# The last 64 keys' values on all 128 rows beside zeros, and every block of 128 tokens through the MLP by itself

## The chip, the cores and the metric

The program runs on one core of one Trainium2 chip. The metric is the device time of one execution in microseconds (us). The engines go by their short names: PE (TensorE; PEld is its weight loads), DVE (VectorE), ACT (ScalarE), POOL (GpSimd), SP (SyncE, which here issues DMAs).

## The reference

Three stages in float32: attention that keeps the 32 largest scores of every row, a SwiGLU MLP behind an RMS norm, and a top-1 mixture of 8 experts.

```python
q, k, v: (4, 8, 576, 64)                       # batch, heads, tokens, head size
scores = q @ k.T / 8;  keep the 32 largest of each row;  attn = softmax @ v
x  = attn as (2304, 512)
xn = x / rms(x) * g
x  = (silu(xn @ w_gate) * (xn @ w_val)) @ w_out            # 512 -> 1536 -> 512
e  = argmax(x @ gate + bias[modality])                     # one of 8 experts per token
out = gate_weight * (relu(x @ w1[e]) @ w2[e])              # 512 -> 1024 -> 512
```

## The kernel before

**Stages.** `front` computes attention and MLP together; `experts` follows. The last MLP output has to be there before the experts start, since the table that says which token goes to which expert is complete only then.

**Tiling of attention.** A sequence of 576 tokens is four blocks of 128 rows (`CM = 4`) and a rest of 64 (`SR`). A *main tile* is 128 query rows of one head. A *rest tile* holds the 64 rest rows of two heads. A *step* takes two tiles, and there are 72 steps, 18 for each of the 4 batches. `PLAN` (line 93) is the order: for batches 0, 1 and 3 the blocks come one at a time, 4 steps for each; in batch 2 blocks 0 and 1 come together, in 8 steps, whose two tiles are the two blocks of one head. "r" stands for the two steps of the rest tiles. Where the two tiles of a step are one block, they are the two heads (`hh` = 0 and 1) of a pair `p`.

**One tile.** `qk` (L530) makes the scores: 4 matmuls, 8 for a rest tile. ACT and DVE copy and halve them (L543 to L547), `topk` (L565, L568) finds the 32 largest on DVE (for each tile four searches for 8 maxima and three removals), `soft1` to `soft3` (POOL L599, ACT) make the weights, `tr` (L625) transposes them, ACT, POOL and DVE write them as two 16-bit halves (`pT` for the 512 main keys, `pr` for the 64 rest keys), and `av` (L671) multiplies them with the values. Float32 is replaced by three 16-bit products (high by high, high by low, low by high); the tiles of pairs 2 and 3 of batch 0 use float32 itself (`whole`).

**The rest keys.** The two tiles of a step lie in one buffer, so that the rest keys of both are neighbours and one transpose (L630) gives `pr` of both: rows 0 to 63 belong to the even tile, rows 64 to 127 to the odd one. So `av` takes 64 rows of `pr` and 64 rows of the values; the 64 rest rows of the values are loaded twice (L388), once for each half. In a rest tile each head's 64 columns are matmuls of their own, with 64 of the array's columns.

**MLP.** A *granule* is one block (or the two blocks of batch 2's first 8 steps; or the rest rows of two batches). Its atoms are `norm`, `xtr`, `ff1` (L750, rows named `pf`: 144 matmuls with w_gate and 144 with w_val for one block), `ff2` (L750, rows named `po`: 72), `route` and `rank` (together some 20 short DVE instructions). A granule of one block streams 128 columns per `ff1` matmul, the granule of two blocks 256 and half as many matmuls for its tokens.

**What sets the order.** Atoms are written into the attention steps by a budget (`mlp_slot`), but a scheduler then orders every engine's instructions by its own simulation of the program. Each engine runs its queue in that order. `w` has 2 buffers and the scores' PSUM tile 1, so a step's scores can be made about one step ahead of the top-k that uses them. `kr` and `vt` share one buffer (tag "raw") outside `whole`.

Of the kernel before, what the change touches and what calls it, by code (L numbers as in the profile page):

```python
# [20 lines left out]
def topk_attention_swiglu_moe_kernel(  # L21
# [192 lines left out]
    def front(exact):  # L214
# [219 lines left out]
        def dma_q(s):  # L434
            qr = ap_.tile([128, 2, D], F32, name="qr", tag="qr", bufs=QB)
            t0, t1 = steps[s]
            b, p, hh, c = t0
            if hh is not None and t1[2] == hh:
                src = q[b, 2 * p + hh, 0:SM, :].rearrange("(p c) d -> p c d", c=CM)
                nc.sync.dma_start(out=qr, in_=src[:, c:c + 2, :])  # L440
            else:
                for t, (b, p, hh, c) in enumerate(steps[s]):
                    if hh is not None:
                        src = q[b, 2 * p + hh, 0:SM, :].rearrange("(p c) d -> p c d", c=CM)
                        nc.sync.dma_start(out=qr[:, t, :], in_=src[:, c, :])
                    else:
                        for i in range(2):
                            nc.sync.dma_start(out=qr[i * SR:(i + 1) * SR, t, :], in_=q[b, 2 * p + i, SM:S, :])
# [905 lines left out]
```

## Time and profile before

| | us |
|---|---|
| median of 3 runs (lowest, highest) | 1242.8 (1239.47, 1243.44) |
| the profiled execution | 1240.91, of it span 1239.3 |
| PE busy in the span | 1138.8 |
| DVE busy | 928.2 |
| ACT busy | 830.5 |
| POOL busy | 731.2 |

The first score matmul of step 18 (batch 1's first) starts at 220.3, that of step 21 at 277.2, that of step 71 (the last) at 803.5; attention's last matmul is at 833.4, the MLP's last at 926.8, and the experts take the rest. The page marks 92% of the span as PE busy, but the ends of matmuls are modelled, so a busy PE need not be one that is kept from starting sooner: the distance between the starts of weight loads shows what each one takes.

### The profile page before, as it was taken

The numbers are of one execution on the slowest core, as the hardware profiler recorded it, in microseconds if no ns is written. First come the engines' busy times: TensorE is split into PE (matmuls) and PEld (weight loads), VectorE is DVE, ScalarE is ACT, GpSimd is POOL, SyncE is SP. The second block draws the span as 40 slices with busy tenths as digits, with TensorE's granted clock in tenths as the row PEclk, the third lists the DMA queues.
The fourth block names the chain that finished last, engine by engine and source line by source line (L and its number), as shares of the span: only waits on it lengthen the run. The fifth ranks groups of instructions, "written<-read, shape, count | busy, mean of one in ns | idle before, by whom it ended". The sixth has DMA issues, their size and how long they took to land. (4 is left out here: it accounts for less than half of the span.)

```text
span 1239.3 us, 32187 instructions
## 1 busy us (share of the span) xinstructions
PE 1138.8 (92%) x12286; PEld 1039.9 (84%) x12286; DVE 928.2 (75%) x2886; ACT 830.5 (67%) x1757; POOL 731.2 (59%) x843
## 2 busy tenths in 40 slices
PE   6976677999999999999999999999997999999994
PEld 6965566888999989999998999999986898798883
DVE  8999999759999999998999999971125526244161
ACT  6868888777888888878888887873333435344260
POOL 7866766858767879867889676564434312222100
PEclk9865676989999999999999999999997999999997
DMA  8242312011000111000011000013006726354230
GB/s 295 51 129 82 100 44 82 13 45 39 21 17 9 32 41 47 24 13 15 17 38 40 28 17 2 11 32 124 11 19 193 247 70 230 128 173 149 66 113 20
DMA packets 69624, 87.54 MB, mean 71 GB/s; under 512 B 34626, under 2 KB 43974, under 8 KB 69448
## 3 DMA queue, kind: packets, MB, share of 16 engines
q1 hardware_dynamic: 62360, 67.86, 17.9%
q0 software_dynamic: 5424, 13.16, 3.3%
q10 hardware_dynamic: 1664, 4.19, 0.9%
q8 instruction: 107, 1.75, 0.6%
q14 instruction: 69, 0.57, 0.2%
HBM read 75.58 MB, written 10.92 MB: 70 GB/s over the span
## 5 line engine op out<-in xcount | busy, mean ns | idle before, releaser
L565 DVE MAX8 w<-w 128x8 f32<-128x296 f32 x576 | 251.9, 462 | 1.2
L599 POOL TENSOR_TENSOR s<-s,r 128x576 f32<-128x576 f32 x144 | 201.1, 1417 | 31.3 <-ACT r L595 31.1
L568 DVE MATCH_REPLACE8 w<-w 128x296 f32<-128x296 f32 x432 | 194.9, 455 | 0.0
L750 PE MATMUL pf<-xT,wg 128*128 128x128 f16 (+1 forms) x2448 | 172.0, 224 | 4.2 <-DVE T L879 2.6
L750 PE MATMUL pf<-xT,wv 128*128 128x128 f16 (+1 forms) x2448 | 167.7, 222 | 0.0
L750 PE MATMUL po<-wo,h 128*128 128x264 f16 (+1 forms) x1296 | 157.4, 275 | 0.9 <-ACT t L777 0.9
L530 PE MATMUL ps<-kS,qS 128*128 128x288 f32 x640 | 138.6, 346 | 20.7 <-DVE w L546 19.6
L750 PEld LDWEIGHTS <-wg 128*128 128x128 f16 x2448 | 148.3, 99 | 11.1 <-issue 4.9
L750 PEld LDWEIGHTS <-wv 128*128 128x128 f16 x2448 | 145.3, 98 | 4.3
L750 PEld LDWEIGHTS <-h 128*128 128x128 f16 x1296 | 122.0, 98 | 18.8 <-issue 1.4
L1137 DVE TENSOR_TENSOR wl<-wr,wh 128x1024 fp32r<-128x1024 f32 x64 | 76.7, 1220 | 66.1 <-ACT wh L1136 66.1
L530 PEld LDWEIGHTS ps<-kS,qS 128*128 128x128 f32 x640 | 104.0, 215 | 23.8 <-ACT r L595 14.9
L603 ACT ACTIVATE s<-s,mbs 128x576 f32<-128x576 f32 x144 | 113.3, 789 | 14.2 <-POOL s L599 13.9
L595 ACT ACTIVATE r<-s,mbs 128x576 f32<-128x576 f32 x144 | 105.0, 781 | 15.1 <-POOL mbs L586 15.0
L625 PE MATMUL pt<-identr,s 128*128 128x128 f32 x576 | 97.6, 300 | 16.9 <-ACT s L603 16.1
L543 ACT COPY s<-ps 128x576 f32<-128x576 f32 x144 | 93.1, 646 | 22.1 <-PE ps L530 21.5
L1243 POOL DMA_INDIRECT out_dram<-o,idx x23 | 23.2, 1010 | 138.0 <-ACT o L1242 106.9
L1184 PE MATMUL ph<-xh,wh 128*128 128x256 f32 x352 | 99.7, 287 | 1.0 <-PEq L1301 1.0
L1184 PE MATMUL ph<-xl,wh 128*128 128x256 f32 x352 | 98.5, 282 | 0.0
L1184 PE MATMUL ph<-xh,wl 128*128 128x256 f32 x352 | 97.1, 284 | 0.8 <-issue 0.8
L782 POOL TENSOR_TENSOR t<-u,t 128x512 f32<-128x512 f32 x54 | 69.6, 1289 | 47.9 <-ACT t L777 30.3
L671 PE MATMUL pt<-vs,pT 128*128 128x64 f16 (+1 forms) x1680 | 88.4, 198 | 8.7 <-POOL pT L639 6.7
(205 smaller groups left out, 2779.0 us busy)
## 6 DMA issues: line engine op xcount, KB each, us to landing
wr<-in_moe_w_dram SPq DMA_DIRECT2D x56, 512.0 KB
wst<-in_moe_w_gate_dram SPq DMA_DIRECT2D x24, 256.0 KB
wst<-in_moe_w_val_dram SPq DMA_DIRECT2D x24, 256.0 KB
kr<-in_k_dram SPq DMA_DIRECT2D x32, 128.0 KB
vt<-in_v_dram SPq DMA_DIRECT2D x32, 128.0 KB
x_d<-xo SPq DMA_DIRECT2D x16, 256.0 KB
wr<-in_moe_w_dram ACTq DMA_DIRECT2D x8, 512.0 KB
qr<-in_q_dram SPq DMA_DIRECT2D x112, 32.0 KB
```

The source lines that it names most:

```text
L530: nc.tensor.matmul(out=ps[:, a, 0:HS], lhsT=qS[i // 2][:, i % 2, j, o2:o2 + 128], rhs=kt[:, m, ks], start=(n == 0), stop=(n == len(ops) - 1),)
L543: nc.scalar.copy(out=s.rearrange("p (a k) -> p a k", a=2), in_=ps[:, :, 0:HS])
L565: steps.append(lambda: dve.max(lists[t][:, 8 * r:8 * r + 8], src[t] if r == 0 else dst[t]))
L568: steps.append(lambda: dve.match_replace(out=dst[t], in_to_replace=lists[t][:, 8 * r:8 * r + 8], in_values=src[t] if r == 0 else dst[t], i ...
L595: nc.scalar.activation(out=d["r"], in_=d["s"], func=AF.Relu, scale=-BIG, bias=d["mb"][:, 1:2])
L599: nc.gpsimd.tensor_tensor(out=d["s"], in0=d["s"], in1=d.pop("r"), op=OP.subtract)
L603: nc.scalar.activation(out=d["s"], in_=d["s"], func=AF.Exp, scale=SCALE, bias=d["mb"][:, 0:1], accum_out=d["rs"])
L625: nc.tensor.transpose(pt[:, c * 128:(c + 1) * 128], e[:, e0 + c * 128:e0 + (c + 1) * 128], ident)
L671: nc.tensor.matmul(out=av_[o:o + n], lhsT=l, rhs=r, start=(a == 0), stop=(a == len(ops) - 1))
L750: nc.tensor.matmul(out=out_, lhsT=l, rhs=r, start=(a == 0), stop=(a == len(ops) - 1))
L1137: nc.vector.tensor_tensor(out=lo, in0=w[0], in1=hi.bitcast(F32), op=OP.subtract)
L1184: nc.tensor.matmul(out=pt, lhsT=l[:, fs], rhs=r[:, kk, :], start=(n == 0), stop=(n == 3 * KD - 1))
```

## The change

1. `dma_v` zeroes 64 rows of the rest keys' values on POOL, per head: head 0 of a pair keeps its values in rows 0 to 63 and zeros below, head 1 the other way round. Each head's 64 rest rows are loaded once.
2. `av` takes all 128 rows of `pr` with all 128 of the values; the other tile's weights meet zeros. For that the tile's place in a step has to be its head's: a main step is always the two heads of a pair, and a rest tile takes head `c` of pair `p` and head `c` of pair `p + 1`.
3. In a rest tile each head's matmuls give all 128 rows, into 64 PSUM columns of their own, and the copy behind them takes the 64 rows that count.
4. `PLAN` has no double block left: 18 granules in place of 17, with 128 columns each.

Places in the queues. PE, step 19, the rest tiles of batch 0 (names: `pt` output, `vs` values, `pT`/`pr` weights of main and rest keys). Before:

```order
L671 LDWEIGHTS pT_3495
L671 MATMUL pt_3487<-vs_593,pT_3495 64x64
L671 LDWEIGHTS pr_3493
L671 MATMUL pt_3468<-vs_332,pr_3493 64x64
L671 LDWEIGHTS pT_3495
```

And now:

```order
L663 LDWEIGHTS pT_3495
L663 MATMUL pt_3487<-vs_593,pT_3495 128x64
L663 LDWEIGHTS pr_3493
L663 MATMUL pt_3468<-vs_593,pr_3493 128x64
L663 LDWEIGHTS pT_3495
```

The two tiles' matmuls still alternate, but every output has 128 rows, and `pr` is read whole.

PE, ahead of the scores (`ps`) of step 18's second tile, the first step of batch 1 (`pf` is an output of `ff1`, `po` one of `ff2`, `h` the hidden values). Before:

```order
L750 LDWEIGHTS wv1_111
L750 MATMUL pf_1676<-xT_1381,wv1_111 128x128
L530 MATMUL ps_3496<-kS_3078,qS_3257 128x288 x4
L625 MATMUL pt_3468<-identr_62,s_3076 128x128 x4
L750 LDWEIGHTS wg0_108
```

And now:

```order
L744 LDWEIGHTS h_1895
L744 MATMUL po_2491<-wo0_112,h_1895 128x264
L524 MATMUL ps_3496<-kS_3078,qS_3257 128x288 x4
L744 LDWEIGHTS h_2181
L744 MATMUL po_2491<-wo0_112,h_2181 128x264
```

Before, 48 `pf` matmuls stand between the scores of the step's two tiles; now 192 `pf` and 12 `po` do, and 61 `po` and 26 of `av` follow before step 19's scores. In the old queue the long run of MLP stands one step later, ahead of step 19's second tile: 144 `pf`, 72 `po` and the rest tiles.

PE, behind attention's last matmul. Before:

```order
L671 LDWEIGHTS pr_12794
L671 MATMUL pt_12788<-vs_10137,pr_12794 128x64
L750 LDWEIGHTS wg0_108
L750 MATMUL pf_15791<-xT_15573,wg0_108 128x128
L750 LDWEIGHTS wg1_109
```

And now:

```order
L663 LDWEIGHTS pr_12803
L663 MATMUL pt_12797<-vs_10146,pr_12803 128x64
L744 LDWEIGHTS h_16346
L744 MATMUL po_16361<-wo1_113,h_16346 128x264
L744 LDWEIGHTS h_16111
```

The old queue has the last 152 `pf` and the 72 `po` of a granule there, the new one only 44 `po` of it; what follows is alike. The MLP matmuls by place in the queue, before and now:

| queued | `pf` 128 columns | `pf` 256 columns | `po` |
|---|---|---|---|
| ahead of step 18's first scores | 48, 96 | 0, 0 | 0, 0 |
| from there to step 21's | 358, 468 | 0, 0 | 72, 72 |
| from there to step 71's | 2979, 3496 | 288, 0 | 864, 936 |
| behind step 71's | 1223, 1124 | 0, 0 | 360, 288 |

On POOL each pair of new zeroing instructions stands behind the split that frees the "raw" buffer, most often directly, and waits for POOL's own semaphore alone; the value DMAs on SP wait for it.

The diff, cut:

```diff
-            if len(cs) == 2:
-                for hh in range(2):
-                    steps.append([(b, p, hh, c) for c in cs])
-            else:
-                steps.append([(b, p, hh, cs[0]) for hh in range(2)])
+            for c in cs:
+                steps.append([(b, p, hh, c) for hh in range(2)])
...
-            steps.append([(b, p, None, None), (b, p + 1, None, None)])
+            steps.append([(b, p, None, hh) for hh in range(2)])
...
-    PLAN = [[[0], [1], [2], [3], "r"], [[0], [1], "r", [2], [3]], [[0, 1], "r", [2], [3]], [[0], [1], "r", [2], [3]]]
+    PLAN = [[[0], [1], [2], [3], "r"], [[0], [1], "r", [2], [3]], [[0], [1], "r", [2], [3]], [[0], [1], "r", [2], [3]]]
...
                 h = 2 * p + i
+                nc.gpsimd.memset(vt[(1 - i) * SR:(2 - i) * SR, i, CM, :], 0.0)
                 nc.sync.dma_start(out=vt[:, i, 0:CM, :], in_=v[b, h, 0:SM, :].rearrange("(p c) d -> p c d", c=CM))
-                for j in range(2):
-                    nc.sync.dma_start(out=vt[j * SR:(j + 1) * SR, i, CM, :], in_=v[b, h, SM:S, :])
+                nc.sync.dma_start(out=vt[i * SR:(i + 1) * SR, i, CM, :], in_=v[b, h, SM:S, :])
...
-            src = q[b, 2 * p + hh, 0:SM, :].rearrange("(p c) d -> p c d", c=CM)
-                nc.sync.dma_start(out=qr, in_=src[:, c:c + 2, :])
...
+                        nc.sync.dma_start(out=qr[i * SR:(i + 1) * SR, t, :], in_=q[b, 2 * (p + i) + c, SM:S, :])
...
-                ops = [(o2, m, j) for o2, m in ([(0, hh)] if hh is not None else [(0, 0), (64, 1)]) for j in range(2)]
+                ks_ = [(0, kS[b, p][:, hh, ks])] if hh is not None else [(64 * m, kS[b, p + m][:, c, ks]) for m in range(2)]
...
-            parts = [(0, 128, hh)] if hh is not None else [(0, 64, 0), (64, 64, 1)]
-            for o, n, h2 in parts:
+            parts = [(0, 128, p, hh)] if hh is not None else [(64 * m, 64, p + m, c) for m in range(2)]
+            for m, (_, _, p2, h2) in enumerate(parts):
...
-                    ks = slice(0, 128) if c2 < CM else slice(r0, r0 + SR)
-                    src, q0 = (pT, c2 * 128 + o) if c2 < CM else (pr, o)
-                    e = [src[ks, a, q0:q0 + n] for a in range(nh)]
+                    e = [pT[:, a, c2 * 128:(c2 + 1) * 128] if c2 < CM else pr[:, a] for a in range(nh)]
...
-                    nc.tensor.matmul(out=av_[o:o + n], lhsT=l, rhs=r, start=(a == 0), stop=(a == len(ops) - 1))
+                    nc.tensor.matmul(
+                        out=d["pt"][:, m * D:(m + 1) * D], lhsT=l, rhs=r, start=(a == 0), stop=(a == len(ops) - 1)
+                    )
...
-                        out=x[x0:x0 + n, hd * D:(hd + 1) * D], in_=av_[o:o + n], func=AF.Copy,
+                        out=x[x0:x0 + n, hd * D:(hd + 1) * D], in_=d["pt"][o:o + n, m * D:(m + 1) * D], func=AF.Copy,
```

## Rows read from the trace of the kernel before

**Rows 1.** The page: busy us (share of the span) and instructions of each engine.

```profile
PE 1138.8 (92%) x12286; PEld 1039.9 (84%) x12286; DVE 928.2 (75%) x2886; ACT 830.5 (67%) x1757; POOL 731.2 (59%) x843
```

**Rows 2.** Busy time by stretch: stretch, length; busy us of PE, PEld, DVE, ACT, POOL; clock.

```profile
100.00:200.00 100.00, 67.29 (x497) 57.98 (x496) 100.00 (x337) 82.88 (x175) 70.80 (x86) 0.69 0.26 73
220.30:277.20 56.90, 53.23 (x645) 47.21 (x644) 38.68 (x134) 41.94 (x97) 39.14 (x44) 0.91 0.11 31
277.20:803.50 526.30, 520.75 (x7029) 482.01 (x7026) 507.25 (x1721) 438.53 (x979) 404.48 (x471) 1.00 0.09 24
803.50:926.80 123.30, 121.39 (x1769) 114.48 (x1767) 40.72 (x181) 51.67 (x110) 56.14 (x58) 1.00 0.14 45
926.80:1239.30 312.50, 280.33 (x1771) 249.08 (x1770) 131.43 (x195) 126.02 (x212) 69.64 (x70) 0.95 0.42 139
```

**Rows 3.** Timeline of weight loads, one main tile: start, us, line, rows*columns, how many.

```profile
402.60 0.50 PEld L671 LDWEIGHTS <-pT 128*128 128x128 f16 x14
403.15 0.14 PEld L671 LDWEIGHTS <-pr 64*128 64x128 f16 x3
403.34 0.73 PEld L750 LDWEIGHTS <-wv 128*128 128x128 f16 x13
```

**Rows 4.** The same view, three loads in a rest tile.

```profile
246.63 0.10 PEld L671 LDWEIGHTS <-pr 64*64 64x64 f16 x1
246.78 0.11 PEld L671 LDWEIGHTS <-pT 128*64 128x64 f16 x1
246.92 0.10 PEld L671 LDWEIGHTS <-pr 64*64 64x64 f16 x1
```

**Rows 5.** The same view, at the first and at the last changes of shape.

```profile
60.73 0.19 PEld L671 LDWEIGHTS <-pr 64*128 64x128 f16 x6
...
833.24 0.14 PEld L671 LDWEIGHTS <-pr 64*128 64x128 f16 x5
833.44 0.45 PEld L750 LDWEIGHTS <-wg 128*128 128x128 f16 x8
```

**Rows 6.** Timeline of PE: pairs of rows whose starts time one MLP matmul.

```profile
403.35 2.63 PE L750 MATMUL pf<-xT,wv 128*128 128x128 f16 x44
405.81 0.37 PE L671 MATMUL pt<-vs,pT 128*128 128x64 f16 x7
...
643.20 2.03 PE L750 MATMUL pf<-xT,wg 128*128 128x256 f16 x17
645.07 0.27 PE L750 MATMUL pf<-xT,wv 128*128 128x256 f16 x1
...
842.85 8.14 PE L750 MATMUL po<-wo,h 128*128 128x264 f16 x72 [0.30 <-ACT t L777]
850.82 0.39 PE L750 MATMUL pf<-xT,wg 128*128 128x128 f16 x4
...
264.65 4.49 PE L750 MATMUL pf<-xT,wg 128*128 128x128 f16 x47
268.98 0.61 PE L625 MATMUL pt<-identr,s 128*128 128x128 f32 x4
```

**Rows 7.** Timeline of DVE, step 19; in brackets the idle time before and who ended it.

```profile
240.35 0.47 DVE L565 MAX8 w<-w 128x8 f32<-128x296 f32 x1
...
250.85 0.17 DVE L809 SCALAR_TENSOR_TENSOR L<-po,mbias 128x8 f32<-128x8 f32 x1 [6.32 <-PE po L750]
...
253.30 0.16 DVE L858 RECIPROCAL gt<-gt 128x1 f32<-128x1 f32 x1
256.83 0.46 DVE L545 TENSOR_TENSOR w<-s,ps 128x288 f32<-128x288 f32 x1 [3.37 <-ACT s L543]
```

**Rows 8.** Busy time by stretch, as in rows 2, before and around that hole.

```profile
200.00:220.00 20.00, 17.01 (x97) 16.02 (x98) 18.33 (x63) 16.06 (x37) 14.29 (x16) 0.66 0.25 71
240.00:258.00 18.00, 16.37 (x153) 13.07 (x154) 3.77 (x19) 10.71 (x31) 9.93 (x12) 1.00 0.07 22
258.00:268.00 10.00, 9.79 (x76) 8.42 (x75) 8.30 (x25) 8.46 (x20) 5.41 (x7) 0.50 0.20 56
```

**Rows 9.** Groups of POOL's instructions by form: count | busy us, mean ns of one.

```profile
L476 POOL MEMSET qS<- 128x256 f32 x8 | 2.5, 317 | 3.7 <-PE ps L530 3.7
L155 POOL MEMSET ones<- 128x128 f16 x1 | 0.2, 205 | 0.0
```

**Rows 10.** SP's DMA issues by line: ns least/median/most, first and last start.

```profile
L440 SPq DMA_DIRECT2D qr<-in_q_dram x8: 327/328/532, 367.2 to 452.0; - x8
...
L388 SPq DMA_DIRECT2D vt<-in_v_dram x64: 465/588/1630, 45.6 to 679.6; - x64
```

More of the change, by code (lines that the diff above doesn't have):

```diff
@@ L435, in dma_q @@
             qr = ap_.tile([128, 2, D], F32, name="qr", tag="qr", bufs=QB)
-            t0, t1 = steps[s]
-            b, p, hh, c = t0
-            if hh is not None and t1[2] == hh:
-                src = q[b, 2 * p + hh, 0:SM, :].rearrange("(p c) d -> p c d", c=CM)
-                nc.sync.dma_start(out=qr, in_=src[:, c:c + 2, :])
[L441 to L448, printed above, removed]
+            for t, (b, p, hh, c) in enumerate(steps[s]):
+                if hh is not None:
+                    src = q[b, 2 * p + hh, 0:SM, :].rearrange("(p c) d -> p c d", c=CM)
+                    nc.sync.dma_start(out=qr[:, t, :], in_=src[:, c, :])
+                else:
+                    for i in range(2):
+                        nc.sync.dma_start(out=qr[i * SR:(i + 1) * SR, t, :], in_=q[b, 2 * (p + i) + c, SM:S, :])
             raw["q", s] = qr
@@ L527, in qk @@
                 ks = slice(o, o + HS)
-                ops = [(o2, m, j) for o2, m in ([(0, hh)] if hh is not None else [(0, 0), (64, 1)]) for j in range(2)]
-                for n, (o2, m, j) in enumerate(ops):
+                ks_ = [(0, kS[b, p][:, hh, ks])] if hh is not None else [(64 * m, kS[b, p + m][:, c, ks]) for m in range(2)]
+                ops = [(o2, kt, j) for o2, kt in ks_ for j in range(2)]
+                for n, (o2, kt, j) in enumerate(ops):
                     nc.tensor.matmul(
-                        out=ps[:, a, 0:HS], lhsT=qS[i // 2][:, i % 2, j, o2:o2 + 128], rhs=kt[:, m, ks],
+                        out=ps[:, a, 0:HS], lhsT=qS[i // 2][:, i % 2, j, o2:o2 + 128], rhs=kt,
                         start=(n == 0), stop=(n == len(ops) - 1),
@@ L653, in av @@
             d = st[i]
[L654 to L656 removed]
+            pT, pr = d["pT"], d["pr"]
             nh = 1 if whole(b, p) else 2
[L658 to L659 removed]
+            parts = [(0, 128, p, hh)] if hh is not None else [(64 * m, 64, p + m, c) for m in range(2)]
+            for m, (_, _, p2, h2) in enumerate(parts):
+                vt = vS[b, p2]
                 ops = []
                 for c2 in range(CM + 1):
[L662 to L664 removed]
+                    e = [pT[:, a, c2 * 128:(c2 + 1) * 128] if c2 < CM else pr[:, a] for a in range(nh)]
                     if nh == 1:
[L666 removed]
+                        ops.append((e[0], vt[:, h2, c2, :]))
                     else:
[L668 removed]
+                        w = [vt[:, a, h2, c2, :] for a in range(nh)]
                         ops += [(e[0], w[0]), (e[0], w[1]), (e[1], w[0])]
                 for a, (l, r) in enumerate(ops):
[L671 removed]
+                    nc.tensor.matmul(
+                        out=d["pt"][:, m * D:(m + 1) * D], lhsT=l, rhs=r, start=(a == 0), stop=(a == len(ops) - 1)
+                    )
             blk, x0 = (b * CM + c, 0) if hh is not None else (NMB + b // 2, (b % 2) * SR)
@@ L677, in post @@
             def post():
-                for o, n, h2 in parts:
-                    hd = 2 * p + h2
+                for m, (o, n, p2, h2) in enumerate(parts):
+                    hd = 2 * p2 + h2
                     nc.scalar.activation(
-                        out=x[x0:x0 + n, hd * D:(hd + 1) * D], in_=av_[o:o + n], func=AF.Copy,
+                        out=x[x0:x0 + n, hd * D:(hd + 1) * D], in_=d["pt"][o:o + n, m * D:(m + 1) * D], func=AF.Copy,
                         scale=d["rs"][o:o + n],
```

6 lines of the change are left out of this document (removed).

## Prediction

> **What bounds the kernel now.** The busy line of the page gives PE 92% of the span and DVE 75% [rows 1]; that is an average over stages, so the stretches come next [rows 2]. From 100 to 200 us DVE is busy all 100 us and PE 67: top-k sets the pace. From 277.2 to 803.5 (steps 21 to 70) PE is busy 520.75 of 526.3 us at full clock and DVE 507.25: two engines at their limit at once, 10.5 us per step. From 803.5 to 926.8 PE alone is full, with what is left of the MLP. From 926.8 the experts run, which the change doesn't touch. So time is to be had from PE between 220 and 927, but between 277 and 803 only as far as DVE can follow: its floor there is 507, that is 19 us below the present length.
>
> The third view is the timeline of weight loads, since starts tell what a matmul takes. In a main tile 14 loads of 128 rows take 0.50 us; with 0.10 for a single one that is (0.50 - 0.10)/13 = 0.031 from start to start. The last of them starts at 403.00, the first 64-row load at 403.15, the last of these at about 403.19, and the next MLP load at 403.34 [rows 3]. So going from 128 rows to 64 takes 0.15 and going back another 0.15, though the three 64-row loads follow each other at 0.02. A rest tile shows the same between its shapes: 246.63, 246.78, 246.92 [rows 4]. From the first change to the last [rows 5] there are 448 changes of shape: 62 before step 18, 48 in steps 18 to 20, 316 in steps 21 to 70, 22 behind. (A main tile has at least two; the rest comes from rest tiles and from tiles that alternate.)
>
> **The change part by part.** *Shapes.* All matmuls become 128 by 128, as many as before. A change of shape costs 0.147 - 0.031 = 0.116; a former 64-row load goes from about 0.015 to 0.031. Steps 18 to 20: 48 x 0.116 - 26 x 0.016 = 5.2 us of PE. Steps 21 to 70: 316 x 0.116 - 330 x 0.016 = 31.4. Behind: 22 x 0.116 - 24 x 0.016 = 2.2. Before step 18 (62 changes, 6 us) DVE is the bound and I count nothing; if it were not full there, up to 6 us more would come.
>
> *Blocks by themselves.* A 128-column `pf` matmul takes (405.81 - 403.35)/44 = 0.056, a 256-column one (645.07 - 643.20)/17 = 0.110, a `po` one (850.82 - 842.85)/72 = 0.111 [rows 6]. 288 x 0.110 = 31.7 become 576 x 0.056 = 32.3: +0.6 on PE. Evictions are of 512 columns either way, as many as before. One more `route` and `rank` costs DVE: the route of one block lasts from 250.85 to 253.46 [rows 7], its own wait for ACT included; with the rank, which runs between other work, I take 2 us.
>
> *Zeros and loads.* 32 zeroings of 64 x 64 on POOL. Not in the trace; a 128 x 128 one took 0.205 us and a 128 x 256 one 0.317 [rows 9], so 0.1 to 0.2 each, 3 to 6 us of POOL over 16 pairs, behind 405 busy us in 526 [rows 2]. Each stands behind the split that freed the buffer and waits only for POOL; behind it in POOL's queue is the next L599 or L639, and SP's value load starts some 0.3 us later, a step ahead of its use. SP loses 32 value loads of 0.588 and gains 8 query loads of 0.328 [rows 10]: 16 us lighter. I count nothing; without that cover it is 0.4 us per pair, 6 us, and as a gain no more than the 3 us by which SP's loads could start sooner.
>
> *Order.* The scheduler pulls MLP forward. With 0.056, 0.110 and 0.111 the queue counts give: behind step 71's first scores 1223 `pf` + 360 `po` = 108.4 before, 1124 + 288 = 94.9 now, so -13.5; in steps 21 to 70 294.4 before, 299.7 now, +5.3; in steps 18 to 20 28.0 before, 34.2 now, +6.2.
>
> *Sum by stage.* Steps 18 to 20 took 56.9 us for some 47 of PE work at full clock (the MLP's 28.0, the attention of three steps at the rate that steps 21 to 70 leave over, 526 - 294 = 232 in 50, and the many changes of their rest tiles). The rest is a hole: DVE ends step 19's first tile at 240.8 and starts the second at 256.83 [rows 7], while 144 `pf`, 72 `po` and the rest tiles pass on PE; then PE ran ten us at the half-rate clock, 0.50 from 258 to 268 [rows 8]. The new queue has the same run one step earlier: 192 `pf` and 12 `po`, 12.1 us, between the scores of step 18's tiles, where DVE has one tile, half of 10.5; then 61 `po` and 26 of `av`, 7.6, and the transposes, before step 19's. Holes of about 7 and 3 us replace one of 16, but PE has 6.2 - 5.2 = 1 us more to do. PE alone would need 48; with another ten us at half rate and the old hole, 66. I take 54: -3.
>
> Steps 21 to 70: PE 520.75 - 31.4 + 5.3 = 494.7, DVE 507.25 + 2 = 509. DVE becomes the bound. Bounds: 509 if it is never kept waiting, as from 100 to 200, and 526 if its waits stay. I take 514: there PE had a third of its time free, here it has 4%, and the queues are in fixed order with about one step of slack; but half the present 19 us of DVE idleness was PE arriving late, and more. -12.
>
> Behind step 71's first scores: -13.5 - 2.2 = -16, bounds -18 and -12, since PE is full there (121.39 of 123.3 [rows 2]) and the experts' first steps are tied to its end.
>
> Together -3 - 12 - 16 = -31. The profiled execution took 1240.9 (span 1239.3 and 1.6 around it), 1.9 below the median of the three; -31 on the median of 1242.8 is **1212**.
>
> **The rivals.**
> *All of PE's saving arrives.* DVE never waits (509) and steps 18 to 20 come near 48: -17 - 8 - 16 = -41, 1202. For it: 100 to 200 us show DVE at 100%. Against: that was with PE a third idle.
> *DVE was the bound already.* Then steps 21 to 70 stay at 526 and only the tail shortens: -16, 1227. For it: DVE is at 96% and many single steps have it full. Against: PE never rests there, and the steps with most matmuls are the longest.
> *The run at step 18 costs more than the old one, and DVE was the bound*: PE does the run at half rate, where a `pf` matmul takes (268.98 - 264.65)/47 = 0.092 [rows 6], so 192 of them 18 us instead of 11, and the old hole stays: +9 (66 for 57), with only the tail's -16 against it: -7, 1236. For it: the mean clock from 200 to 220 is 0.66 [rows 8]. Against: PE is given more to do there, not less.
> *The clock falls (slower).* PE is no longer always full in steps 21 to 70 and drops to half rate as it did at 258 [rows 8]. Each ten-us stretch loses 5 us of PE work. PE's 494.7 has to grow past 526.3 + 19 = 545 before the kernel is slower: 51 us lost, so from the eleventh stretch on. At 15 of them 494.7 + 75 = 570: +44 - 19, 1268. For it: between 100 and 200, with PE at 67%, the mean clock is 0.69. Against: at half rate PE is full, and full it stays fast, as from 277 to 803; there is always MLP to fill it.
> *The change doesn't do what it says.* The 0.15 us could be the wait for `pr` to be written, not the change of shape. Then they stay, and the 380 former 64-row loads cost 6 us more: PE-bound, 1242.8 + 6 = 1249. For it: the jump always stands at `pr`. Against: it stands on the way back too, ahead of MLP loads that have long been ready [rows 3, 5], and between `pT` loads [rows 4].
> The Trainium skill speaks against the change here: its page "TensorE: Matmul & The Clock Gate", Part 3 (packing small matmuls), has short contractions run beside each other when each lies in its own row group, and puts the gain in using such tiles. By that the change gives up a fast path (0.02 instead of 0.031, as rows 3 show for the three loads themselves), and the time would be this rival's. Another page of the Trainium skill, "TensorEngine Tiling (Array Packing)", Key Properties, has a change of tiling mode drain the engine; by that the jumps go. The trace has three fast loads between two jumps and so sides with the second.
>
> **How the numbers follow.** Forecast (1205 to 1221) 0.52; all of it 0.14; DVE bound already 0.18; step 18's run 0.06; clock 0.06; shape not the cause 0.04. The range takes forecast, all-of-it and the tail-only case with their spread: 1198 to 1233, which leaves out the last three, 0.16, and a little at the edges. Faster by over 0.3% (3.7 us, about what a measurement of this kernel tells from none): 0.52 + 0.14 + 0.18 = 0.84 and a third of the fourth, 0.86; the other two thirds same, 0.04, and with 0.01 from the tail-only case's upper edge 0.05; slower 0.06 + 0.04 = 0.10, less 0.01 that the last two leave within 0.3%, 0.09.
>
> **What would show it.** No weight load of 64 rows or columns, and starts 0.03 apart right through `av`. Steps 21 to 70 in about 514 us with DVE at 99% and PE below 97% busy by starts; if DVE stays at 96% the tail-only case holds. Step 71's scores to the MLP's end 107 instead of 123.3. Around step 18 two DVE holes of 7 and 3 us instead of 16. The granted clock 1.00 from step 21 on; any 0.5 there speaks for the clock. It would be wrong if jumps of 0.15 remain at `pr`, or if DVE, full, is slower per instruction than now.

## The result and the profile after

The changed kernel takes 1225.2 us (median of 4 runs, 1223.8 to 1226.6) beside 1241.1 for the kernel before in the same comparison: ratio 0.9871, interval 0.9845 to 0.9896, so 16 us faster. I had forecast 1212 with a range of 1198 to 1233. The sign and the range held; half of the forecast gain is missing.

The page of the kernel after has, where [rows 1] had 92% for PE and 75% for DVE:

```profile
PE 1110.3 (91%) x12573; PEld 1032.5 (84%) x12573; DVE 942.6 (77%) x2904; ACT 829.1 (68%) x1758; POOL 738.0 (60%) x875
```

PE has lost 28.5 us of busy time, DVE has gained 14.4. The stretches answer to [rows 2]. The bounds are again the first score matmuls of steps 18, 21 and 71 and the MLP's end, which from here on is the start of the first matmul behind the MLP: 910.7 here, 926.5 before (the columns are stretch, length, busy us of PE, PEld, DVE, ACT, POOL, clock):

```profile
100.00:200.00 100.00, 71.86 (x478) 63.55 (x477) 98.17 (x328) 80.67 (x169) 69.62 (x84) 0.60 0.26 73
224.20:284.00 59.80, 54.24 (x757) 51.65 (x757) 43.47 (x126) 43.75 (x103) 44.73 (x53) 0.97 0.10 28
284.00:802.30 518.30, 500.68 (x7339) 474.85 (x7337) 514.19 (x1760) 440.04 (x988) 412.04 (x495) 1.00 0.09 24
802.30:910.70 108.40, 105.61 (x1595) 100.39 (x1593) 39.80 (x159) 45.28 (x98) 47.38 (x47) 1.00 0.15 51
910.70:1222.40 311.70, 280.19 (x1775) 249.19 (x1773) 131.38 (x196) 126.19 (x212) 70.53 (x70) 0.96 0.42 139
```

Read the third row first. In steps 21 to 70 PE and DVE have changed places: before, the stage was 5.6 us longer than PE's busy time and 19 longer than DVE's; now it is 4.1 longer than DVE's and 17.6 longer than PE's. The list of what PE waits for in this stage (line, who releases it: us in all, times, longest) has 11.2 us of waits for DVE, and had 3.6 before. Two of the rows before, from 277.2 to 803.5, the longest and the one for the scores:

```profile
PE pf L750 <- DVE u L772: 1.2, 1, 1.2
PE ps L530 <- DVE w L546: 0.4, 1, 0.4
```

After, from 284.0 to 802.3, the score matmuls wait for DVE to have read the scores before them:

```profile
PE ps L524 <- DVE w L540: 4.1, 11, 0.6
PE pt L663 <- DVE pT L635: 2.7, 5, 1.2
```

The jumps of [rows 3 to 5] are gone. In a stretch of `av` with loads for the rest keys (`pr`) among the others, starts now follow at 0.02 to 0.03 us, also on the way out:

```profile
422.28 0.10 PEld L663 LDWEIGHTS <-pr 128*128 128x128 f16 x1
422.31 0.10 PEld L663 LDWEIGHTS <-pT 128*128 128x128 f16 x1
422.33 0.10 PEld L663 LDWEIGHTS <-pr 128*128 128x128 f16 x1
...
422.45 0.16 PEld L663 LDWEIGHTS <-pr 128*128 128x128 f16 x3
422.54 0.57 PEld L524 LDWEIGHTS ps<-kS,qS 128*128 128x128 f32 x4
```

What made DVE the longer one is in its short operations. In steps 21 to 70 before (count | busy us, mean ns), then after, where each line number is 6 lower:

```profile
L882 DVE TENSOR_TENSOR T<-T,O 128x8 f32<-128x8 f32 x10 | 8.3, 829 | 0.0
L855 DVE TENSOR_TENSOR O<-iota,mx 128x8 f16<-128x8 f32 x10 | 3.0, 298 | 0.0
L847 DVE TENSOR_TENSOR d<-L 128x8 f32<-128x8 f32 x10 | 2.2, 215 | 0.0
```

```profile
L849 DVE TENSOR_TENSOR O<-iota,mx 128x8 f16<-128x8 f32 x13 | 9.0, 694 | 0.0
L876 DVE TENSOR_TENSOR T<-T,O 128x8 f32<-128x8 f32 x12 | 6.7, 558 | 0.0
L841 DVE TENSOR_TENSOR d<-L 128x8 f32<-128x8 f32 x13 | 4.4, 336 | 0.0
L873 DVE TENSOR_TENSOR T<-pr,ecol 128x8 f32<-128x8 f32 x12 | 1.8, 151 | 0.0
```

L873 does as much work as L876 and takes 0.14 to 0.17 us every time; it reads PSUM (`pr` is here the rank's PSUM tile). The three with operands in SBUF alone together took 13.5 us and now take 20.1; a single L876 takes anything from 0.14 to 1.41 us. The timeline shows a long one: DVE's rows first, then POOL's (a pair of 2.80 us, and the next).

```profile
606.16 1.34 DVE L876 TENSOR_TENSOR T<-T,O 128x8 f32<-128x8 f32 x1
607.42 0.46 DVE L559 MAX8 w<-w 128x8 f32<-128x296 f32 x1
```

```profile
604.67 2.80 POOL L593 TENSOR_TENSOR s<-s,r 128x576 f32<-128x576 f32 x2
607.41 1.18 POOL L778 TENSOR_TENSOR h<-t,h 128x512 f16<-128x512 f32 x1
```

POOL's pair ends at 607.47 and DVE's operation at 607.50. I added up, for all DVE operations before the attention's end, what each took above the shortest of its line and shape, where that was over 0.15 us. Before: 28 operations, 19.1 us. After: 42 operations, 31.7 us; 33 of them end within 0.05 us after a POOL operation, as 6% of all DVE operations of steps 21 to 70 do. The other nine are all L395, and each ends 0.34 to 0.36 us after a POOL operation. I call this DVE's held-up time below; in steps 21 to 70 alone it went from 18.5 to 25.0 us. The largest single one is an L395, the scaling of a value tile, in steps 18 to 20 (before, the two in this stage had a mean of 0.48 us). DVE, then POOL:

```profile
268.38 5.10 DVE L395 TENSOR_SCALAR vt<-vt 128x640 f32<-128x640 f32 x1 [2.64 <-ACT vs L394]
273.40 0.67 DVE L766 SCALAR_TENSOR_TENSOR u<-u,pf 128x512 f32<-128x512 f32 x1
```

```profile
267.95 1.25 POOL L885 DMA_INDIRECT tab_d<-pay,si  x1 [0.19 <-issue]
269.23 2.78 POOL L593 TENSOR_TENSOR s<-s,r 128x576 f32<-128x576 f32 x2
271.97 1.15 POOL L778 TENSOR_TENSOR h<-t,h 128x512 f16<-128x512 f32 x1
273.56 1.40 POOL L396 TENSOR_TENSOR vs<-vt,vs 128x640 f16<-128x640 f32 x1 [0.43 <-DVE vt L395]
```

It ends 0.36 us after the first moment at which POOL rests. That it has to wait for such a rest is not shown: each of the other eight L395 ends so after one POOL operation, some of them while POOL goes straight on.

By stage the sum reads: step 18 starts 3.9 us later (forecast 0); steps 18 to 20 +2.9 (forecast -3); steps 21 to 70 -8.0 (forecast -12); from there to the MLP's end -14.6 (forecast -16); the experts -1.1. Together -16.9.

### The profile page after: what moved, and what is told of

It reads as the page before. It is cut to its first block, busy times and chain, and to the rows that moved or that the text cites. A ratio compares the mean times of both kernels' runs of the same rounds, so it can differ in the third digit from the quotient of the medians.

```text
span 1222.4 us, 32736 instructions
## 1 busy us (share of the span) xinstructions
PE 1110.3 (91%) x12573; PEld 1032.5 (84%) x12573; DVE 942.6 (77%) x2904; ACT 829.1 (68%) x1758; POOL 738.0 (60%) x875
## 5 line engine op out<-in xcount | busy, mean ns | idle before, releaser
L744 PE MATMUL pf<-xT,wg 128*128 128x128 f16 x2592 | 170.9, 221 | 4.3 <-DVE T L873 1.8
L744 PE MATMUL pf<-xT,wv 128*128 128x128 f16 x2592 | 169.4, 219 | 0.5 <-ACT xf L733 0.3
L744 PEld LDWEIGHTS <-wg 128*128 128x128 f16 x2592 | 152.2, 99 | 6.4 <-issue 3.5
L744 PEld LDWEIGHTS <-wv 128*128 128x128 f16 x2592 | 149.9, 98 | 4.1 <-issue 1.8
L524 PEld LDWEIGHTS ps<-kS,qS 128*128 128x128 f32 x640 | 105.7, 219 | 31.0 <-ACT r L589 16.9
L537 ACT COPY s<-ps 128x576 f32<-128x576 f32 x144 | 93.2, 647 | 21.2 <-PE ps L524 20.1
L663 PE MATMUL pt<-vs,pT 128*128 128x64 f16 x1680 | 80.1, 197 | 13.1 <-POOL pT L633 7.1
## 6 DMA issues: line engine op xcount, KB each, us to landing
wr<-in_moe_w_dram ACTq DMA_DIRECT2D x8, 512.0 KB, 10.2
```

The source lines that it names most:

```text
L524: nc.tensor.matmul(out=ps[:, a, 0:HS], lhsT=qS[i // 2][:, i % 2, j, o2:o2 + 128], rhs=kt, start=(n == 0), stop=(n == len(ops) - 1),)
L537: nc.scalar.copy(out=s.rearrange("p (a k) -> p a k", a=2), in_=ps[:, :, 0:HS])
L663: nc.tensor.matmul(out=d["pt"][:, m * D:(m + 1) * D], lhsT=l, rhs=r, start=(a == 0), stop=(a == len(ops) - 1))
L744: nc.tensor.matmul(out=out_, lhsT=l, rhs=r, start=(a == 0), stop=(a == len(ops) - 1))
```

## The experiments

Twelve kernels ran. The table puts their stages side by side; each has its text below. "Held up" is DVE's time as defined above. "MLP" is what the queue holds of the MLP in steps 21 to 70 and behind them, by its counts and the prediction's 0.056, 0.110 and 0.111 us. Bounds and busy times are read from each trace as above; the traced execution is 6 us shorter than the median in e1_blocks and e2_main64, and within 3 us of it in the others. The tail runs from step 71's first scores to the MLP's end.

| kernel | median us | step 18 starts | 18-20 | 21-70 | PE, DVE busy there | tail | held up | MLP |
|---|---|---|---|---|---|---|---|---|
| before | 1241.1 | 220.3 | 57.0 | 526.3 | 520.7, 507.2 | 123.0 | 19.1 | 294, 108 |
| e1_blocks | 1257.4 | 218.7 | 57.5 | 532.6 | 524.2, 510.2 | 127.3 | 22.4 | 291, 112 |
| e3_before_less | 1238.4 | 206.9 | 53.8 | 522.6 | 517.3, 482.1 | 140.4 | 22.7 | 285, 124 |
| after | 1225.2 | 224.2 | 59.8 | 518.3 | 500.7, 514.2 | 108.4 | 31.7 | 300, 95 |
| e8_shapes | 1227.9 | 223.5 | 60.3 | 518.6 | 498.7, 512.8 | 111.5 | 31.0 | 298, 96 |
| e3_after_less | 1218.8 | 216.7 | 62.1 | 487.6 | 470.8, 480.0 | 137.4 | 33.2 | 270, 124 |
| e2_main64 | 1242.4 | 224.5 | 50.5 | 531.9 | 519.2, 521.2 | 116.7 | 31.5 | 300, 102 |
| e5_route | 1223.2 | 225.9 | 59.8 | 510.0 | 491.7, 504.6 | 114.7 | 23.0 | 293, 102 |
| e10_psum | 1243.6 | 225.9 | 59.2 | 500.3 | 477.3, 489.4 | 141.6 | 7.5 | 274, 121 |
| e6_both | 1220.3 | 223.7 | 51.0 | 503.0 | 489.7, 493.7 | 127.9 | 10.8 | 292, 115 |
| e7_ahead | 1239.7 | 226.2 | 56.9 | 530.5 | 507.6, 522.7 | 111.0 | 35.4 | 304, 98 |
| e9_slot | 1275.4 | 227.5 | 61.7 | 588.3 | 541.2, 534.9 | 85.1 | 27.2 | 319, 67 |
| e12_route_hp0 | 1224.5 | 226.2 | 64.8 | 506.5 | 492.6, 503.1 | 109.1 | 15.6 | 295, 96 |
| e13_qr13 | 1229.2 | 226.4 | 59.8 | 520.0 | 499.6, 515.5 | 108.9 | 32.5 | 300, 94 |

**Which part of the change it was.** First each part alone. e1_blocks:

```diff
-    PLAN = [..., [[0, 1], "r", [2], [3]], ...]
+    PLAN = [..., [[0], [1], "r", [2], [3]], ...]
```

> The kernel before with one edit: in the plan of the third batch the two blocks that passed the MLP as a pair pass it one by one. All shapes stay as they were, the jumps of 0.15 us too. Theory (the shapes carry the gain, the blocks nothing): the queue has 291 us of MLP matmuls in steps 21 to 70 where it had 294, and 4 more behind them, so within 3 us of the kernel before, 1238 to 1245. Rival (the gain comes from the new order that single blocks bring): at least half of the 16 us, 1225 to 1233.

Measured: 1257.4 us, ratio 1.0127 (1.0098 to 1.0156). Slower by 15 us, outside both expectations. In its profiled run, the shortest of four, 10 us are in sight: steps 21 to 70 are 6.3 longer and the tail 4.3; 30 more changes of shape in steps 21 to 70 (345 where before has 315) are 3.5 us of that, 6.8 us at half the clock there (0.50 granted from 549.0 to 552.4 and from 682.1 to 685.5; none before) some 3 more, less 3 us of MLP that left the stage; 4 more us of MLP are the tail. The rest stays open. In the old shapes single blocks are no gain of their own, that much is shown.

e8_shapes is the opposite, all of the change but the blocks:

```diff
-    PLAN = [..., [[0], [1], "r", [2], [3]], ...]
+    PLAN = [..., [[0, 1], "r", [2], [3]], ...]
```

> The changed kernel with the pair of blocks back in the third batch's plan; all loads stay 128 by 128. Theory (the shapes carry the gain): as the changed kernel, 1221 to 1229, with one route less on DVE. Rival (the blocks or the order carry it): back towards the kernel before, 1233 to 1241.

Measured: 1227.9 us, ratio 0.9895 (0.9859 to 0.9931): the changed kernel within 3 us. The shapes carry the gain (the zeros come with them; e2_main64, next, keeps the zeros and loses the gain).

e2_main64 keeps the new rest tiles and gives main tiles their 64-row loads back:

```diff
-                    e = [pT[...] if c2 < CM else pr[:, a] for a in range(nh)]
+                    kr = slice(0, 128) if c2 < CM or hh is None else slice(i % 2 * SR, i % 2 * SR + SR)
+                    e = [pT[...] if c2 < CM else pr[kr, a] for a in range(nh)]
...
-                        w = [vt[:, a, h2, c2, :] for a in range(nh)]
+                        w = [vt[kr, a, h2, c2, :] for a in range(nh)]
```

> The changed kernel with one part of the change taken back: in main tiles the rest keys' loads are of 64 rows again (the zeros stay, unused there); rest tiles keep 128. At least two jumps of 0.15 us come back in each of the 88 main tiles of steps 21 to 70: 176 x 0.116 less 264 x 0.016 is 16 us more for PE there, 4 in the other stages. The queue also holds 8 us more of the MLP behind step 71's scores and 5 less in steps 18 to 20. Theory (the jumps are what was paid; DVE is full in the changed kernel, so PE's 17 us of idle time there absorb part): steps 21 to 70 in 522 to 530 us where they took 518.3, in all 1229 to 1238. Rival (the rest tiles' changes of shape were the costly ones, those in main tiles lie in PE's waits): steps 21 to 70 as now, in all 1224 to 1230 by the MLP's order alone.

Measured: 1242.4 us, ratio 1.0003 (0.9976 to 1.0029), slower than either expected. The jumps are back, 222 in steps 21 to 70 with a median of 0.146 us from start to start, as in this main tile:

```profile
408.25 0.44 PEld L664 LDWEIGHTS <-pT 128*128 128x128 f16 x12
408.74 0.14 PEld L664 LDWEIGHTS <-pr 64*128 64x128 f16 x3
408.93 0.40 PEld L421 LDWEIGHTS pk<-identr,ks 128*128 128x128 f32 x4
```

The stage takes 531.9, above the 522 to 530 expected, and two engines press on it:

```profile
224.50:275.00 50.50, 47.40 (x654) 44.91 (x653) 35.01 (x117) 41.21 (x95) 36.70 (x47) 0.98 0.11 29
275.00:806.90 531.90, 519.20 (x7400) 486.24 (x7397) 521.18 (x1751) 440.45 (x985) 412.26 (x494) 1.00 0.09 23
```

PE is 18.5 us busier there than in the changed kernel (16 expected), so the jumps in main tiles are real time; and DVE is 7 busier, 4 of it held-up time (29.0 in the stage beside 25.0). In steps 18 to 20, which have no change of shape left in this kernel and 28.8 us of MLP (before: 28.0), the stage is 50.5 where it was 57.0, and PE's busy time 47.4 where it was 53.2: 5.8 less, where the prediction counted 5.2 for the shapes. But the clock differs too, 0.98 here and 0.91 before: before, PE ran 10.2 us there at half rate, here 2.3. With that time counted half, PE's 5.8 are about 2, and 3 with the 0.8 us of MLP; the shapes' 5.2 is not shown by this stage.

**Whether PE or DVE sets the length.** e3_before_less and e3_after_less each have one edit, which leaves out the third removal of maxima:

```diff
-                if r < 3:
+                if r < 2:
                     drop(0, r)
                     drop(1, r)
```

> The kernel before without the third of the three removals of eight maxima in each row (so the last eight maxima are taken from a row that still holds the third eight: this part of the top-k is left out). DVE loses 63 us in all, some 44 of them in steps 21 to 70. It makes PE the bound from step 21 on, with the shapes of before. Theory (PE's counted saving of some 35 us from step 21 to the MLP's end is real, and DVE kept the changed kernel from having all of it): here 16 us less before step 18, where DVE sets the pace, a few in steps 18 to 20, and nearly nothing from step 21 to the MLP's end beyond the 6 us by which PE was not busy: 1215 to 1225. Rival (DVE set the pace of before in steps 21 to 70 as well): 44 us more come off, below 1200.

> The changed kernel without the third removal of eight maxima, as in the run beside it (this part of the top-k is left out). Both are bound by PE from step 21 to the MLP's end, so their difference there is what the shapes alone give to PE, whatever the order of the MLP. Theory (0.116 us for each of some 340 changes of shape, less 0.016 for each former 64-row load): 30 to 36 us less from step 21 to the MLP's end than the run beside it, and in all 1183 to 1192. Rival (the changes of shape were worth half of what I counted, and DVE was not what held the changed kernel back): 12 to 20 us less, 1198 to 1210.

Measured: 1238.4 and 1218.8 us. The totals lie 13 and 27 us above the ranges expected, for one reason that I had not thought of: less MLP stands in the steps and more behind them (column MLP), so what a stage gains the tail pays (+17 and +29 us). I take it that with less DVE work the planner thinks the steps shorter. The stages still answer the question:

```profile
260.70:783.30 522.60, 517.30 (x6897) 476.65 (x6898) 482.11 (x1521) 435.47 (x974) 400.72 (x468) 0.99 0.08 23
```

```profile
278.80:766.40 487.60, 470.75 (x6914) 446.95 (x6914) 479.97 (x1528) 425.83 (x963) 396.49 (x479) 1.00 0.09 24
```

The first is before without the third removal: DVE loses 25 us, the stage 4. PE set the length. The second is after without it: DVE loses 34, the stage 31. But PE loses 30 there too, by 29 us of MLP that moved out, so this loss alone does not tell the two apart; that DVE is the nearer bound even with a third of the removals gone rests on the 7.6 us that DVE stands in this stage and the 16.9 that PE does. The pair also gives the shapes' worth on PE whatever the order: from step 21 to the MLP's end PE is busy 654.7 us in the one and 605.5 in the other, 49.2 less, and 15.0 of that is MLP that its queue holds less there; 34.2 are the shapes. The same working gives 33.5 for e1_blocks against after, 27.8 for before against e8_shapes, 27.3 for before against after. Part of this spread is the clock: PE was busy 8.8, 6.4 and 3.4 us at half rate in e3_before_less (262.1 to 268.9 and 344.0 to 347.4), e1_blocks and e8_shapes (730.3 to 733.7), and not at all in the other three. With that time counted half, the four are 29.8, 30.3, 29.5 and 27.3. I had counted 31.4 + 2.2 = 33.6.

**What holds DVE up.** e5_route writes the small operations with one full operand and a scalar per row, and has fewer of them:

```diff
-                nc.vector.tensor_tensor(out=T, in0=L, in1=bc(mx), op=OP.is_equal)
-                nc.vector.tensor_tensor(out=T, in0=T, in1=be(iota8), op=OP.mult)
+                m1 = mx[:, 0:1]
+                nc.vector.scalar_tensor_tensor(out=T[:, 0], in0=L[:, 0], scalar=m1, in1=iota8, op0=OP.is_equal, op1=OP.mult)
...
-                nc.vector.tensor_tensor(out=O, in0=be(iota8), in1=bc(mx), op=OP.is_equal)
+                nc.vector.tensor_scalar(out=O[:, 0], in0=iota8, scalar1=m1, scalar2=None, op0=OP.is_equal)
...
-                    nc.vector.tensor_tensor(out=acc_oh, in0=acc_oh, in1=O[:, j, :], op=OP.add)
+                    nc.gpsimd.tensor_tensor(out=acc_oh, in0=acc_oh, in1=O[:, j, :], op=OP.add)
...
```

> The changed kernel with the route's and the rank's short DVE operations rewritten: one operand of most of them becomes a scalar per row (comparison, difference), the finiteness test multiplies by 0 in one operation, one addition moves to POOL and one to a small matmul. DVE has some five fewer operations of 128 by 8 with two inputs per block. Theory (the short operations with two inputs in SBUF are held up by POOL's elementwise operations, 32 us in the changed kernel where it was 19 before): the time lost so falls to 15 to 20 us (what L395 and the rest lose), DVE's busy time in steps 21 to 70 falls from 514 to 500 to 506 and their length with it to 505 to 510; the queue moves 7 us of MLP behind step 71's scores, so in all 1217 to 1224. Rival (POOL holds DVE up as often, only in other operations): DVE's lost time stays above 28, its busy time above 510, in all 1227 to 1233.

Measured: 1223.2 us, ratio 0.9832 (0.9802 to 0.9862). DVE's busy time (504.6), the stage (510.0) and the total are as the theory had them; the held-up time is 23.0, more than the 15 to 20 expected. What is left shows why: scalar forms that read SBUF are held up too, while the product with the PSUM tile is not.

```profile
L850 DVE TENSOR_SCALAR O<-iota,mx 128x8 f16<-128x8 f32 x12 | 7.7, 641 | 0.0
L843 DVE TENSOR_SCALAR d<-L 128x8 f32<-128x8 f32 x12 | 6.1, 508 | 0.0
L875 DVE TENSOR_TENSOR T<-pr,O 128x8 f32<-128x8 f32 x12 | 1.8, 152 | 0.0
```

So e10_psum moves the operands into free columns of PSUM tiles and leaves the operations, but for the finiteness test, which has one in place of two, and one addition, which goes to POOL:

```diff
-                            rt["L"] = mp.tile([128, 2, E], F32, name="L", tag="L", bufs=1)[:, 0:nb]
+                            rt["x"] = [pt[:, o:o + E].unsqueeze(1) for o in range(272, 304, E)]
+                            rt["L"] = rt["x"][0]
...
-                    T = mp.tile([128, 2, E], F32, name="T2", tag="T2", bufs=1)[:, 0:nb]
+                    T = rt["pr"][:, E:2 * E].unsqueeze(1)
...
```

> The changed kernel with the route's and the rank's small operands laid in free columns of the PSUM tiles that the MLP's output and the rank already have: as many DVE operations (one fewer), but none of 128 by 8 with two inputs in SBUF, and the one addition that would have two moves to POOL. Theory (a short DVE operation with its inputs in SBUF waits for the POOL operation beside it; with an operand in PSUM it doesn't): the time that DVE loses so falls from 31.7 to 9 to 14 us (the rest is L395), DVE's busy time in steps 21 to 70 from 514 to 490 to 498, and the stage from 518.3 to 494 to 503. The tiles are held longer, so the queue moves 26 us of MLP behind step 71's scores: the tail 132 to 136 where it took 108.4, in all 1224 to 1236. Rival (where the operands lie doesn't matter, POOL holds up whatever DVE runs): DVE's lost time stays above 22, the stage above 508, in all 1238 or more.

Measured: the held-up time is 7.5 us, all of it L395. The same operations as above, in the names that they have here (`po` and `pr` are PSUM tiles):

```profile
L850 DVE TENSOR_TENSOR O<-iota,po 128x8 f16<-128x8 f32 x11 | 1.6, 149 | 0.0
L877 DVE TENSOR_TENSOR pr<-pr,O 128x8 f32<-128x8 f32 x11 | 1.7, 157 | 0.0
L842 DVE TENSOR_SCALAR po<-po 128x8 f32<-128x8 f32 x11 | 1.8, 161 | 0.0
```

The stage is 500.3 (494 to 503 expected), DVE 489.4. The rival is out: it does matter where the operands lie. The total is not as expected, 1243.6 us (ratio 1.0020, 1.0004 to 1.0036), and lies where the rival had it, for another reason: the tail takes 141.6, of which PE is busy 133.1. I had sized the tail by MLP alone; PE stands 8.5 us there, 2.8 in the tail of after. That the route holds the tiles longer would explain it, but is not shown.

e6_both is e5_route with L395 on ACT:

```diff
-                nc.vector.tensor_scalar(out=vt, in0=vt, scalar1=SV, scalar2=None, op0=OP.mult)
+                nc.scalar.activation(out=vt, in_=vt, func=AF.Copy, scale=SV)
```

> The changed kernel with the route rewritten as in the run with scalars per row, and L395, the scaling of the values, on ACT and not on DVE. The queue moves 10 us of MLP out of steps 18 to 20, and 20 more lie behind step 71's scores than in the changed kernel. Theory (of the 3 to 7 us that the part before step 21 became longer, 5 are the L395 that POOL held up for 5.1 us in step 19): steps 18 to 20 in 51 to 55 us where they took 59.8, DVE's lost time from 23 to 13 to 16, steps 21 to 70 in 496 to 506, the tail in 126 to 130: in all 1214 to 1226. Rival (that L395 lay beside a wait for PE and costs nothing): steps 18 to 20 in 57 or more in spite of the 10 us of MLP that leave them, in all 1227 to 1234.

Measured: 1220.3 us, ratio 0.9832 (0.9806 to 0.9857), 5 us under the changed kernel and the shortest of those that do the whole work. Its rows as above:

```profile
223.70:274.70 51.00, 46.69 (x603) 43.98 (x604) 38.49 (x127) 45.56 (x107) 40.95 (x50) 0.97 0.11 29
274.70:777.70 503.00, 489.74 (x7287) 467.19 (x7284) 493.66 (x1685) 438.21 (x989) 407.38 (x503) 1.00 0.10 25
777.70:905.60 127.90, 125.69 (x1876) 119.69 (x1877) 41.56 (x162) 53.53 (x113) 60.59 (x65) 1.00 0.13 43
```

Held up are 10.8 us, less than the 13 to 16 expected. Steps 18 to 20 are 8.8 shorter, but 9.7 us of MLP have left them: that L395's 5.1 us lengthened them is not shown by this.

**The run at step 18, and the order.** e7_ahead raises one priority:

```diff
-                    new.append(ahead(HP, qk, nxt[QR.index(r)]))
+                    new.append(ahead(1000 if i < 20 else HP, qk, nxt[QR.index(r)]))
```

> The changed kernel with a higher priority for the score matmuls up to step 19 alone, which puts 48 and not 192 pf matmuls and 12 po ahead of the scores of step 18's second tile, and splits step 19's run about its second tile's scores (75 and 69). Theory (that run at step 18 keeps DVE waiting and costs what the old hole had cost): steps 18 to 20 in 53 to 56 us where the changed kernel took 59.8, and step 18 starts up to 3 us sooner; the queue moves 5 us of MLP into steps 21 to 70 and 3 behind them: in all 1217 to 1224. Rival (the run costs nothing of its own, the stage is as long as its work): steps 18 to 20 stay at 59 to 61, in all 1226 to 1233.

Measured: 1239.7 us, ratio 0.9972 (0.9953 to 0.9990): neither. Steps 18 to 20 take 56.9, 2.9 less, with 5.5 us less MLP in them; step 18 starts later, not sooner. So the run did not cost what I had put on it, unless the clock hid it: its mean is 0.87 in the stage where the changed kernel has 0.97, for it was at half rate from 264.7 to 274.9. And steps 21 to 70 are 12 us longer:

```profile
226.20:283.10 56.90, 53.17 (x653) 50.65 (x652) 39.12 (x126) 44.38 (x99) 39.18 (x49) 0.87 0.09 27
283.10:813.60 530.50, 507.57 (x7439) 480.20 (x7435) 522.72 (x1747) 438.21 (x986) 413.55 (x496) 1.00 0.09 23
```

Here too the stage follows DVE (8.5 busier than in after). 7.3 of that is held-up time (32.3 in this stage beside 25.0), and DVE stands 7.8 us where it stood 4.1; that is 11 of the 12 us.

e9_slot lets the planner hand out more MLP at a time:

```diff
-        MLP_SLOT = 1.3 if exact else 0.35
+        MLP_SLOT = 1.3 if exact else 1.0
```

> The changed kernel with one number changed: the planner hands out MLP work in portions of 1.0 and not 0.35, which puts more of it into the steps: by the queue's counts 19 us more in steps 21 to 70, 3 in steps 18 to 20, 5 before step 18, and 28 us less behind step 71's scores. Theory (DVE is full in steps 21 to 70 and PE has 17.6 us of idle time there, so that much MLP fits in without lengthening them): steps 21 to 70 in 520 to 528 us, the tail in 80 to 84 where it took 108.4, in all 1203 to 1213. Rival (PE's idle time is of a kind that no MLP fits into, since longer runs keep DVE waiting): what leaves the tail comes back in the steps one to one, in all 1222 to 1228.

Measured: 1275.4 us, ratio 1.0245 (1.0219 to 1.0271), worse than the rival. The tail falls to 85.1, near the count, but the steps grow by 70 for 19 us of MLP. With pieces of up to 10.8 us between scores (5.4 in the changed kernel), DVE stands 53 us (its row, then what it waits for and one such wait):

```profile
289.20:877.50 588.30, 541.24 (x7709) 509.07 (x7709) 534.88 (x1789) 452.81 (x1010) 416.12 (x495) 0.97 0.07 21
```

```profile
DVE w L539 <- ACT s L537: 18.6, 14, 4.9
DVE u L766 <- ACT u L765: 10.3, 5, 4.0
DVE pr L639 <- ACT pr L637: 7.3, 4, 3.8
```

```profile
317.58 0.46 DVE L539 TENSOR_TENSOR w<-s,ps 128x288 f32<-128x288 f32 x1 [4.87 <-ACT s L537]
```

The clock has a share as well: 0.97, with PE busy 28.7 us at half rate, some 14 us of work lost. Idle time of PE next to a full DVE is thus no room for MLP in pieces of this size.

e12_route_hp0 is e5_route with `HP` 0 for 500.

> The route with scalars per row, and the planner without its lead for scores, transposes and av (priority offset 0 where it is 500), which leaves 6 us less of MLP behind step 71's scores than the route alone and puts 3 each into steps 18 to 20 and 21 to 70, in no longer pieces. Theory (in steps 21 to 70 DVE sets the length, so MLP that goes there costs nothing as long as its pieces stay under some 6 us): steps 21 to 70 in 505 to 513, the tail in 107 to 111, in all 1211 to 1223, the shortest of all. Rival (a new order by itself costs what the run with scores first up to step 19 showed, 10 us and more of waits): 1230 to 1240.

Measured: 1224.5 us, ratio 0.9863 (0.9827 to 0.9899). Steps 21 to 70 (506.5) and the tail (109.1) are as expected: beside e5_route the stage has 2.6 us more MLP and is 3.5 shorter, 3.3 of which is held-up time, so MLP in small pieces goes into a stage that DVE bounds without lengthening it. But steps 18 to 20 take 64.8, with 37 us of MLP, and the experts 6 us longer than in the changed kernel; 3.4 us more at half rate there (1021.7 to 1025.1) are some 2 of the 6, and for the rest I have no reason. The total just misses the theory's range.

e13_qr13 asks what a new order is worth by itself:

```diff
-        QR = (1, 4)
+        QR = (1, 3)
```

> The changed kernel with the scores of each step's second tile handed to the planner one slot earlier, a change that leaves the amounts of MLP in every stage within 0.6 us of the changed kernel and its pieces as long. It shows how much a new order by itself moves the time. Theory (stage lengths follow DVE's work, and the order matters only by what it moves between stages and by how often POOL holds DVE up): 1221 to 1230. Rival (order alone is worth more than this change's parts): outside 1216 to 1234.

Measured: 1229.2 us, ratio 0.9900 (0.9872 to 0.9928), 4 us above the changed kernel with the same MLP in every stage and 0.8 us more held-up time. That is the size below which a total can't be put down to any one cause here; e7_ahead shows that a new order, with the MLP that it moves, can cost 14.

## Why the prediction was right in part, step by step

**Shapes: right, and a little too large.** That 128-row loads take the jumps away, and that these are time of PE, is shown by the loads, by e8_shapes against e1_blocks, by e2_main64, where the jumps come back and PE is 18.5 us busier, and by PE's busy time: 27 to 34 us less in four comparisons, 27 to 30 with the half-rate clock allowed for, 33.6 counted. The rival of another cause, 1249, is out: in this kernel the two jumps cost more than the short loads between them gain.

**Steps 21 to 70: the mechanism right, DVE's term too small.** That DVE becomes the bound was the forecast, and the step from its busy time to the stage held: 514 - 509 = 5 us of idleness, measured 4.1. The 509 failed. DVE is busy 514.2: the prediction added 2 us for one more route, priced by the one route in [rows 7], where no operation was held up, and took the rest as fixed. The extra route was not the part that failed: e8_shapes, which has the old number of routes, still has 512.8. What grew is held-up time, 25.0 us in this stage where it was 18.5, and all of that in the small operations (21.4 and 13.8; L395 loses 3.6 and lost 4.7). e10_psum shows the cause of the long ones. Why more of them meet POOL in the new order is only argued: a DVE that never rests has no gap in which POOL is idle too. The prediction's last sentence, DVE slower per instruction, is what came. PE's term was off as well, 494.7 counted and 500.7 measured (with the MLP as counted, the shapes gave 25.4 here and not 31.4), but PE no longer set the length.

**Behind step 71's scores: right.** -14.6 for a forecast of -16, by MLP that the queue holds less.

**Steps 18 to 20: wrong.** Forecast -3, measured +2.9. The step that failed is that two holes of 7 and 3 us replace one of 16: they did not come. DVE stood 16.3 us of this stage (59.8 - 43.5), in pieces of 2.6 us at most, and 18.2 before. e7_ahead removed the run that I blamed, and the stage gave 2.9 with 5.5 us less MLP. The other term, "PE alone would need 48", was too small: PE is busy 54.2 us, 3.4 of them at half rate (256.1 to 259.5), so by my estimate 52.5 at full clock. Of that 34.2 are MLP, as counted, and 18.3 the rest, where the sum had 13.8; the shapes' 5.2 is not shown in this stage. The held-up L395 lies there as well; its share was not isolated.

**Before step 18: nothing was counted, and 3.9 was lost.** Every kernel with 128-row loads throughout starts step 18 at 216.7 or later, and at 223.5 or later with all removals; those with the old shapes and all removals start at 218.7 to 220.3. The jumps are not what decides it, for e2_main64, which has them in its main tiles, starts at 224.5. Most of it is work moved, not added: DVE is busy 213.7 of the 224.2 us, and was 210.1 of 220.3, so it stands as long as before (10.5 and 10.2). Ahead of its first operation of step 18, DVE's queue has, from step 12 on, 39 match_replace, 62 maxima and 32 conversions where it had 35, 60 and 29. What sets this order is the planner; I did not test it. The zeros took POOL 0.146 us each, as estimated (0.1 to 0.2), but no run leaves them out, so what they do to the order is open.

**The rivals.** All of PE's saving arrives: out, PE has 17.6 us without work in steps 21 to 70. DVE was the bound already (1227): the total is near it, but not by its sum, since the stage fell from 526.3 to 518.3 and e3_before_less shows PE as the bound of before. The run at step 18 at half rate: the stage took 59.8, not 66, with 3.4 us at half rate. The clock: 1.00 in steps 21 to 70, out.

**Where the expected gain went.** PE's work fell by 27 to 30 of the 33.6 us counted; 12 us of that turned into PE standing in steps 21 to 70 (5.6 us before, 17.6 now; its waits for DVE went from 3.6 to 11.2), and 7 were given back before step 21. Making DVE faster did not bring them back by itself: e5_route takes 8 us off the stage and 6 go to the tail, e10_psum 18 and 33. The queue holds 7 and 26 us more MLP there; that the planner moves it by its own idea of the steps' length is argued, not shown.

## What to carry to other kernels

Where two engines are within 4% of a stage, price both after the change, and price the second one's small operations by their group's mean and spread, not by one quiet row. Look at whether DVE's short operations with operands in SBUF end together with POOL's long ones: an operand in PSUM, or another engine, took that wait away here. With a planner in between, work saved on an engine can move other work; read stages and what the queue puts into them before believing a total.

## What the hardware showed that I had not expected

A DVE operation of 0.15 us takes up to 1.4 when a POOL operation on SBUF runs beside it, and one L395 took 5.1, through four POOL operations in a row; the same operations with an operand in PSUM took a mean of 0.149 to 0.161, and none over 0.18 (e10_psum, steps 21 to 70). The Trainium skill, page "SBUF — State Buffer", section "Who interferes with whom", says that a DVE instruction with two inputs in SBUF contends with POOL's reads and that the pair of ports is held for a whole instruction. This case agrees, with 1.34 us for L876. The same section of the Trainium skill lets tensor_scalar contend too, in some of its modes; in e5_route it did, with a mean of 0.641 us for L850. In which mode these ran, no trace here shows.
